# Later probabilities turned on TensorE, keys and values ahead of q, landings over both queues, a last product in two banks

## The chip, the cores and the metric

The kernel runs on one core of one Trainium2 chip. The metric is device time in microseconds of one execution; the median over runs counts. The engines have the profile's names: PE (TensorE, matrix products; PEld is its loading of weights), DVE (VectorE), ACT (ScalarE), POOL (GpSimd) and SP (SyncE, which here only issues transfers). Matrix products go into eight accumulation banks of 512 columns of 32-bit floats, from where DVE or ACT move them to on-chip memory; POOL cannot read the banks.

## The reference

All in 32-bit floats. First a linear attention, then a mixture of four experts in which every token goes through every expert.

```python
# attention: q, k, v are (8, 8, 576, 64)
kv  = np.einsum('bhsd,bhse->bhde', k, v)
out = np.einsum('bhsd,bhde->bhse', q, kv)
rms = np.sqrt(np.mean(out * out, axis=-1, keepdims=True) + 1e-06)
x   = out / rms * g_norm            # then (B, S, H*D) -> x: (4608, 512)

# experts: domain_probs (4608, 4), w1 (4, 512, 1024), w2 (4, 1024, 512)
p = domain_probs / (domain_probs.sum(-1, keepdims=True) + 1e-09)
for e in range(4):
    h = np.maximum(x @ w1[e], 0.0)
    out += p[:, e:e + 1] * (h @ w2[e])
```

## The kernel before

**Tiles and stages.** The 4608 tokens are nine chunks of 512: chunk `b` below 8 holds 512 tokens of batch `b`, the ninth the 64 left over from each of the eight batches. A step `s = 9 e + i` takes one chunk through one expert, so there are 36 steps. `opening` (L876) computes the attention of batch 0, `attention` (L1041) that of batches 1 to 7, one in each step of the first expert. The products of a step are `up` (x times w1) and `down` or `down_deep` (h times w2). They are written in Winograd's form of Strassen's scheme, seven products of half-size blocks instead of eight, in two levels where time allows; so DVE and POOL form sums and differences of weights and activations (`combine`, recorded at L579), ACT copies or negates, and half-products are merged from the banks. All matrix products of the steps are recorded at L556, in `halves_of`.

**Order of the work.** Nothing is ordered by the program text. Each piece of work is given to a planner (`Plan`, L44) by `plan.add`, with a key (about when), a cost for each engine that can do it, and its buffers. `layout` then simulates the core with these costs, once, when the kernel is built: it picks for every engine in turn the ready piece that is due first, and gives out buffers and banks as they become free. The order that results is the program, one queue for each engine, in which every instruction waits for all before it. In the simulation, `begin` (L352) reckons when a transfer lands: SP's transfers share one queue (`self.bus`), POOL's another (`self.bus_pool`), and neither knows of the other. `DEALS` is a table of draws for each step: each draw shifts the due times of some pieces at random, by a fixed generator, so another table is another order.

**The pieces that the change touches.** `norm_probs` (L592) loads the probabilities, four numbers (16 bytes) for each token, into `p_all`, with a token's block in the partition where the merge needs it. `load_first` takes those of chunk 0, `load_all` (L604 to L610) the rest, with seven transfers issued by POOL; `norm` (L613) divides by the sums. In `opening`, the four pairs of heads are loaded one after another by SP, q, then k, then v (L891). Four turns of q (L907), the product of keys and values (`key_values`, L918) and the turn of the ninth part of q (L926, in the same piece as the key and value product) lead to `attend` (L963). The weights of a later expert are loaded by SP; six of an expert's sums are started by ACT with a negated copy (`subtract_from`, L649, its ACT copy at L653), upon which POOL adds the other addend by a transfer that accumulates. `result` (L1588) gives `merge`, which scales half a product by a probability and adds it to the accumulator (on DVE at L1641, on ACT at L1633), and `send`, which writes a finished block to the output (L1657 by POOL, L1659 by SP). In the last step (`ends` in `down`, L1670) the last products go through a bank of kind `ab` with their merges behind them. At the start, while nothing is there to compute, PE runs products of the identity with itself (L1961).

## Time and profile before

| | |
|---|---|
| median of 3 runs | 1637.3 us (1635.74 to 1640.91) |
| the profiled execution | 1635.26 us, its span 1633.5 us |
| TensorE busy | 1622.3 us, 99% of the span |
| VectorE, ScalarE, GpSimd busy | 82%, 60%, 37% |
| transfers issued by SP (q1) | 199.96 MB, 40.3% of 16 engines' span |
| transfers issued by POOL (q0) | 36.78 MB, 15.0% |

The span runs from the first to the last instruction. A row of a group or of the order of time gives the engine, the line, the operation, tile written <- tiles read (buffer numbers left out), the shape and, after an x, how many instructions; in square brackets stands how long the engine was idle before, and whose work ended it. In the order of time the first two figures are start and duration in us; an instruction of PE counts until its result is out, so those that follow one another overlap in duration. `u`, `db`, `ab` are banks, `big`, `small`, `kv`, `xa`, `xb`, `w1y`, `w2y`, `w2e`, `snap` on-chip buffers.

### The profile page before, as it was taken

The numbers are of one execution on the slowest core, as the hardware profiler recorded it, in microseconds if no ns is written. First come the engines' busy times: TensorE is split into PE (matmuls) and PEld (weight loads), VectorE is DVE, ScalarE is ACT, GpSimd is POOL, SyncE is SP. The second block draws the span as 40 slices with busy tenths as digits, with TensorE's granted clock in tenths as the row PEclk, the third lists the DMA queues.
The fourth block names the chain that finished last, engine by engine and source line by source line (L and its number), as shares of the span: only waits on it lengthen the run. The fifth ranks groups of instructions, "written<-read, shape, count | busy, mean of one in ns | idle before, by whom it ended". The sixth has DMA issues, their size and how long they took to land.

```text
span 1633.5 us, 66413 instructions
## 1 busy us (share of the span) xinstructions
PE 1622.3 (99%) x28876; PEld 1555.9 (95%) x28876; DVE 1334.2 (82%) x2185; ACT 975.8 (60%) x2473; POOL 603.8 (37%) x581
## 2 busy tenths in 40 slices
PE   9999999999999999999999999999999999999999
PEld 5599888989999999999999999999999999999997
DVE  5877787888887987877988887878888887877876
ACT  4455655565566665665666666665566566666653
POOL 4111324232343545433454543332354533333333
PEclk9999999999999999999999999999999999999999
DMA  9977888653764435444676454344577544444442
GB/s 231 217 190 204 227 223 196 179 175 153 230 178 127 119 99 151 118 118 105 183 181 146 107 127 118 97 113 114 141 187 178 127 116 107 118 108 116 118 105 54
DMA packets 225598, 240.99 MB, mean 148 GB/s; under 512 B 100890, under 2 KB 165274, under 8 KB 225306
## 3 DMA queue, kind: packets, MB, share of 16 engines
q1 hardware_dynamic: 201690, 199.96, 40.3%
q0 software_dynamic: 23616, 36.78, 15.0%
q8 instruction: 227, 3.72, 0.9%
q14 instruction: 65, 0.53, 0.1%
HBM read 162.21 MB, written 74.47 MB: 145 GB/s over the span
## 4 chain that ended last, share of the span: by engine, by line
PE 97%; DMA 2%; SPq 0%; ACT 0%; issue 0%; DVE 0%; POOL 0%; DVEq 0%; ACTq 0%; POOLq 0%
PE u L556 47%; PE db L556 30%; PE ab L556 16%; PE ab L1113 1%; DMA big<-in_moe_w_dram 1%; PE ab L1138 1%; DMA big<-in_v_dram 1%; PE ab L1181 0%; DMA big<-roots 0%; SPq L585 0%; PE db L1138 0%; PE u L922 0%; PE ab L1961 0%; DMA kv<-in_v_dram 0%; PE db L963 0%
## 5 line engine op out<-in xcount | busy, mean ns | idle before, releaser
L579 DVE TENSOR_TENSOR big<-big,big 128x1024 f32<-128x1024 f32 (+1 forms) x572 | 537.8, 953 | 31.8 <-ACT big L1447 13.0
L556 PE MATMUL db<-big,big 128*64 128x128 f32 (+1 forms) x5344 | 400.4, 286 | 1.3 <-DVE big L579 0.7
L556 PEld LDWEIGHTS db<-big,big 128*64 128x64 f32 x5344 | 315.5, 137 | 22.1 <-ACT big L1633 2.1
L1491 DVE TENSOR_TENSOR big<-u,snap 128x256 f32<-128x256 f32 x460 | 193.6, 421 | 135.3 <-PE u L556 87.8
L1483 ACT ACTIVATE snap<-u 128x256 f32<-128x256 f32 x490 | 187.5, 383 | 165.1 <-PE u L556 134.2
L579 POOL TENSOR_TENSOR big<-big,big 128x256 f32<-128x256 f32 (+1 forms) x155 | 179.3, 1159 | 249.6 <-DVE big L579 150.5
L1483 ACT ACTIVATE big<-u 128x256 f32<-128x256 f32 x460 | 174.9, 383 | 74.2 <-PE u L556 54.6
L556 PE MATMUL u<-xa,big 128*64 128x128 f32 x2784 | 206.9, 273 | 0.0
L556 PE MATMUL u<-xb,big 128*64 128x128 f32 x2688 | 198.8, 273 | 0.0
L579 POOL TENSOR_TENSOR big<-big 128x512 f32<-128x512 f32 (+1 forms) x88 | 106.0, 1205 | 245.9 <-DVE big L579 136.7
L556 PE MATMUL u<-xa,w1y 128*64 128x128 f32 x2232 | 168.3, 273 | 1.8 <-ACT u L1483 1.8
L556 PEld LDWEIGHTS u<-xa,big 128*64 128x64 f32 x2784 | 163.4, 137 | 1.6 <-ACT big L1163 0.4
L556 PE MATMUL u<-xb,w1y 128*64 128x128 f32 x2208 | 164.7, 273 | 0.0
L1812 ACT ACTIVATE snap<-db 128x256 f32<-128x256 f32 (+1 forms) x256 | 91.6, 358 | 117.6 <-PE db L556 99.7
L556 PEld LDWEIGHTS u<-xb,big 128*64 128x64 f32 x2688 | 157.3, 137 | 0.1
L1447 ACT ACTIVATE big<-big 128x1024 f32<-128x1024 f32 x133 | 140.2, 1054 | 8.5 <-DVE big L579 7.5
L556 PEld LDWEIGHTS u<-xa,w1y 128*64 128x64 f32 x2232 | 131.1, 137 | 5.5 <-ACT u L1483 2.0
L556 PEld LDWEIGHTS u<-xb,w1y 128*64 128x64 f32 x2208 | 129.4, 137 | 0.5 <-DVE big L1641 0.4
L1820 DVE TENSOR_TENSOR big<-ab,snap 128x256 f32<-128x256 f32 x188 | 79.0, 420 | 61.9 <-ACT snap L1812 31.0
L1657 POOL DMA_DIRECT2D out_dram<-big x124 | 108.2, 1217 | 37.3 <-ACT big L1633 28.3
L579 DVE TENSOR_TENSOR big<-big 128x512 f32<-128x512 f32 (+1 forms) x155 | 116.6, 758 | 2.5 <-ACT big L1447 1.8
L1483 ACT ACTIVATE u<-u 128x256 f32<-128x256 f32 x245 | 90.9, 372 | 40.2 <-PE u L556 29.0
(244 smaller groups left out, 2849.6 us busy)
## 6 DMA issues: line engine op xcount, KB each, us to landing
xb<-x SPq DMA_DIRECT2D x44, 512.0 KB, 3.7
xa<-x SPq DMA_DIRECT2D x40, 512.0 KB, 3.5
out_dram<-big POOLq DMA_DIRECT2D x76, 256.0 KB, 6.1
big<-in_moe_w_dram SPq DMA_DIRECT2D x30, 512.0 KB, 5.8
w2e<-x SPq DMA_DIRECT2D x20, 512.0 KB, 3.9
xa<-x_h SPq DMA_DIRECT2D x37, 256.0 KB, 3.1
x_h<-big SPq DMA_DIRECT2D x18, 512.0 KB, 5.6
x<-xb SPq DMA_DIRECT2D x18, 512.0 KB, 4.5
```

The source lines that it names most:

```text
L556: nc.tensor.matmul(out_[cols], lhsT=lhsT[:, cols], rhs=rhs, **kw)
L579: lambda eng: adder(eng).tensor_tensor(out=out_(), in0=a(), in1=b(), op=op),
L1113: nc.tensor.matmul(bank.ap[o * D:(o + 1) * D, r * D:(r + 1) * D], lhsT=ks[r], rhs=vs[r], start=(j == r == 0), stop=(j == len(sets[0]) - 1) ...
L1138: nc.tensor.matmul(to[o].ap[cols, 0:width], lhsT=kv.ap[half, cols], rhs=qt.ap[half, r * S + at_:r * S + at_ + width],)
L1447: lambda eng: nc.scalar.activation(out=b.ap[:], in_=b.ap[:], func=ACT.Relu),
L1483: lambda eng: nc.scalar.activation(out=where(), in_=ps.ap[:, 0:HN], func=ACT.Copy),
L1491: lambda eng: nc.vector.tensor_tensor(out=block(whole, a, t), in0=src.ap[:, 0:HN], in1=add_.ap[:], op=ALU.add),
L1657: nc.gpsimd.dma_start(out=dst, in_=cell(i)[parts, :], accum_op=ALU.add)
L1812: lambda eng: nc.scalar.activation(out=where(), in_=group_of(ps.ap), func=ACT.Copy),
L1820: lambda eng: nc.vector.tensor_tensor(out=cell(tq, dq), in0=group_of(src.ap), in1=group_of(add_.ap), op=ALU.add,),
```

## The change

- **Probabilities.** Those of chunks 1 to 8 are loaded as 32 rows of 128 tokens (2 KB each) into a buffer of kind `big`: four transfers of seven rows (`load_rows`) and three for the four rows of left-over tokens (`load_ends`), all issued by POOL in two pieces. PE turns the rows, one transpose for each expert (`turn_all`), into a bank of kind `ab`, and DVE copies them to their places in `p_all` with five copies (`place_all`). `norm` follows as before.
- **Opening.** The loads of a pair of heads are issued as k, v, q. The planned sizes in the table beside them keep their places. The turn of the last part of q is a piece of its own, after the key and value product; the product no longer waits for q.
- **Landings.** In the simulation, a transfer on one queue is charged 1.2 times the time in which work of the other queue is under way beside it (`TOGETHER`), on both sides.
- **Last product.** In the last step, the second set of last products (t = 1) that use the first bank (m = 1, 6, 7) is cut into two of 128 columns, each in a bank of its own, with merges of 128 columns. The planned cost of a merge on DVE follows the width.
- **Draws.** The table `DEALS` is another one.

```diff
-    RATE, RATE_POOL, OPEN, MARGIN = 260.0, 130.0, 36.0, 1.0
+    RATE, RATE_POOL, OPEN, MARGIN, TOGETHER = 260.0, 130.0, 36.0, 1.0, 1.2
     DEALS = {
-        -3: (61,), -2: (115, 312), -1: (33, 472, 740, 903, 1097), 0: (62, 254, 593, 971, 1064), 1: (203,
...
+        -3: (139, 366), -2: (169, 421, 503, 934), -1: (223, 416, 853, 1011), 0: (151, 283, 537, 780, 1204),
...
         if eng == "SP":
-            self.bus = max(self.bus, t + 1.5) + op.kb / (215.0 if t < self.OPEN else self.RATE)
+            work = op.kb / (215.0 if t < self.OPEN else self.RATE)
+            self.bus = max(self.bus, t + 1.5) + work
+            if t >= self.OPEN:
+                self.bus += self.TOGETHER * min(max(0.0, self.bus_pool - self.bus + work), work)
...
             if op.kb:
-                self.bus_pool = max(self.bus_pool, op.end + 2.0) + op.kb / self.RATE_POOL
+                work = op.kb / self.RATE_POOL
+                other = min(max(0.0, self.bus - op.end - 2.0), work)
+                self.bus_pool = max(self.bus_pool, op.end + 2.0) + work + self.TOGETHER * other
...
-        def load_all(eng):
-            nc.gpsimd.dma_start(out=p_all[0:REM, B * NR, :], in_=first[:, S // D - 1, :])
-            nc.gpsimd.dma_start(
-                out=p_all[0:REM, B * NR + 1:NBLK, :], in_=by_batch[NT:S, 2::2, :])
-            nc.gpsimd.dma_start(out=p_all[REM:P, B * NR:NBLK, :], in_=by_batch[NT:S, 1::2, :])
-            for r in range(NR):
-                nc.gpsimd.dma_start(
-                    out=p_all[:, NR + r:B * NR:NR, :], in_=by_batch[r * P:(r + 1) * P, 1:, :])
+        def load_rows(eng):
+            t = rows_.ap[0:late, 0:P * E]
+            for r in range(NR):
+                nc.gpsimd.dma_start(
+                    out=t[r * (B - 1):(r + 1) * (B - 1), :],
+                    in_=whole[1:, r * P * E:(r + 1) * P * E])
+
+        def load_ends(eng):
+            ends, n = rows_.ap[NR * (B - 1):late, 0:P * E], REM * E
+            nc.gpsimd.dma_start(out=ends[:, n:], in_=whole[1::2, NT * E:])
+            nc.gpsimd.dma_start(out=ends[1:, 0:n], in_=whole[2::2, NT * E:])
+            nc.gpsimd.dma_start(
+                out=ends[0:1, 0:n].rearrange("p (x e) -> p x e", e=E),
+                in_=first[:, S // D - 1, :].unsqueeze(0))
+
+        def turn_all(eng):
+            t = rows_.ap[0:late, 0:P * E].rearrange("p (x e) -> p e x", e=E)
+            for e in range(E):
+                nc.tensor.transpose(
+                    bank.ap[:, e * late:(e + 1) * late], t[:, e, :], ident[0:late, 0:late])
+
+        def place_all(eng):
+            got = bank.ap[:, 0:late * E].rearrange("p (e n) -> p n e", e=E)
+            at = NR * (B - 1)
+            nc.vector.tensor_copy(out=p_all[:, B * NR:NBLK], in_=got[:, at:late])
+            for r in range(NR):
+                made = nc.vector.tensor_copy(
+                    out=p_all[:, NR + r:B * NR:NR], in_=got[:, r * (B - 1):(r + 1) * (B - 1)])
+            return made
...
-        plan.add(key + 0.8, {"POOL": 5.6}, load_all, writes=[probs_later], kb=72, after=opened, lands=5.5)
+        plan.add(key + 0.8, {"POOL": 3.5}, load_rows, parts=[rows_], kb=64, after=opened, lands=4.0)
+        plan.add(key + 0.9, {"POOL": 2.7}, load_ends, parts=[rows_], kb=16, after=opened, lands=4.0)
+        plan.add(key + 1.0, {"PE": 0.35}, turn_all, reads=[rows_], writes=[bank]).turns = True
+        plan.add(key + 1.1, {"DVE": 0.8}, place_all, reads=[bank], writes=[probs_later])
...
-            for t, src, kb in zip("qkv", (q, k, v), (
+            for t, src, kb in zip("kvq", (k, v, q), (
                     (172, 194, 290), (183, 150, 150), (237, 400, 150), (172, 150, 172))[hp]):
...
-                nc.tensor.transpose(bank[1].ap[0:D, P:2 * P], qt.ap[:, (J - 1) * D:J * D], ident[:])
-
-            turned = plan.add(
-                at(hp), {"PE": 1.28}, key_values, reads=[qt, kt, vt], writes=kbank)
+
+            turned = plan.add(at(hp), {"PE": 1.14}, key_values, reads=[kt, vt], writes=kbank)
             turned.turns = True
-            left_q = Buf(None, f"ql{n}")
+            left_q, turned_q = Buf(None, f"ql{n}"), Buf(None, f"qlt{n}")
+            plan.add(
+                at(hp), {"PE": 0.14},
+                lambda eng, bank=kbank, qt=qt: nc.tensor.transpose(
+                    bank[1].ap[0:D, P:2 * P], qt.ap[:, (J - 1) * D:J * D], ident[:]),
+                reads=[qt], writes=[turned_q], parts=kbank[1:], after=[turned]).turns = True
...
-                    key, {"DVE": 0.5},
+                    key, {"DVE": 0.14 + 0.0014 * (cols.stop - cols.start)},
...
+                cut = (P, P) if ends and t else (HN,)
                 if m == 1:
-                    banks[1] = Buf(kind, f"d1_{s}_{t}")
+                    banks[1] = [Buf(kind, f"d1_{s}_{t}_{w}") for w in range(len(cut))]
...
+                pieces = [
+                    (ps, slice(w * n, (w + 1) * n)) for w, (ps, n) in enumerate(zip(banks[1], cut))
+                ] if m in (1, 6, 7, 4) else [(banks[2], slice(0, HN))]
+
+                for ps, cols in pieces:
+                    wide = cols.stop - cols.start
...
```

More of the change, by code (lines that the diff above doesn't have):

```diff
@@ L1609, in rows, with cell @@
             ]
-        def cell(i, half=None):
+        def cell(i, half=None, cols=slice(0, HN)):
             at = (i % 2) * DM
@@ new lines, in down, with product @@
+                for ps, cols in pieces:
+                    wide = cols.stop - cols.start
+                    def product(eng, m=m, t=t, ps=ps, cols=cols, wide=wide):
+                        for kt in range(4):
+                            halves_of(
+                                ps.ap[:, 0:wide], four(h[m])[:, kt // 2, t, kt % 2, :],
+                                rhs=w2f[e][m].ap[:, kt * HN + cols.start:kt * HN + cols.stop],
+                                start=(m in (1, 2, 5) and kt == 0), stop=(kt == 3),
+                                skip_group_check=True,
+                            )
+                    op = plan.add(
+                        key, pe(4, wide), product, reads=[h[m], w2f[e][m], w2corner[e][m]],
+                        writes=[ps],
+                        after=(second[-1:] if m in (1, 5) and not ends else []) + firsts[t:t + 1],
+                    )
+                    op.marks, op.opens = (ps, wide), m == 1
+                    if m == 1 and cols.stop == HN:
+                        firsts.append(op)
+                    if m == order[-1]:
+                        second.append(op)
+                    to = [{
+                        1: (t, 0, True), 2: (t, 0, False), 6: (t, 1, True), 3: (t, 1, False),
+                        5: (2 + t, 1, True), 7: (2 + t, 1, 5 not in order), 4: (2 + t, 0, True),
+                    }[m]]
+                    if mixed and m == 5:
+                        to.append((t, 1, False))
+                    if mixed and m == 7:
+                        to.append((2 + t, 0, True))
+                    for i, half, fresh in to:
+                        merge(
+                            key - 0.4, [ps], lambda ps=ps, wide=wide: ps.ap[:, 0:wide], i, half,
+                            fresh, cols=cols)
```

42 lines of the change are left out of this document (9 added, 33 removed), and 10 rows, old and new, of the table DEALS.

## The prediction

> **What bounds the kernel now.** I read the page's busy times first, then the list of waits of TensorE, then busy time by stage, and last the order of time at the places where TensorE waits.
>
> ```profile
> PE 1622.3 (99%) x28876; PEld 1555.9 (95%) x28876; DVE 1334.2 (82%) x2185; ACT 975.8 (60%) x2473; POOL 603.8 (37%) x581
> ```
>
> TensorE is busy for 1622.3 of 1633.5 us. The arithmetic stays, so only the idle 11.2 us, and work of TensorE that is none, can be won. The waits (engine, line, what it waited for, total, times, longest):
>
> ```profile
> PE u L556 <- ACT u L1483: 1.8, 1, 1.8
> PE ab L1113 <- DMA big<-in_v_dram: 1.4, 1, 1.4
> PE ab L1961 <- POOL ident masks.py:199: 1.4, 1, 1.4
> PE u L556 <- DVE big L1491: 1.1, 1, 1.1
> PE db L556 <- DVE big L579: 0.7, 1, 0.7
> PE db L556 <- ACT big L1633: 0.6, 1, 0.6
> PE db L963 <- DVE kv L940: 0.3, 1, 0.3
> ```
>
> Seven waits, 7.3 us; nearly all the rest of the 11.2 lies behind the last matmul. By stage (after the stretch and its length stand the busy times of PE, PEld, DVE, ACT and POOL):
>
> ```profile
> 50.00:60.00 10.00, 10.00 (x132) 5.11 (x124) 9.81 (x19) 2.32 (x7) 0.00 (x0) 1.00 0.67 204
> 1200.00:1600.00 400.00, 399.98 (x7328) 399.70 (x7325) 323.95 (x519) 248.97 (x629) 154.77 (x145) 1.00 0.48 123
> ```
>
> In the late 400 us TensorE is never without work. In order of time the waits stand, as the rows below show, in the first 80 us and, one of them, at 857 us. So the answer is a sum over a few places.
>
> **1. Probabilities as rows.** Removed: seven POOL transfers, four of them (L610) in pieces of 16 bytes. Beside them stand loads of keys and values, before and during (KB each, median us from issue to landing):
>
> ```profile
> big<-in_k_dram SPq DMA_DIRECT2D x1, 240.0 KB, 4.2
> big<-in_v_dram SPq DMA_DIRECT2D x2, 240.0 KB, 8.4
> L610 POOL DMA_DIRECT2D p_all<-in_moe_domain_probs_dram x4: 943/952/995, 30.7 to 33.6; - x4
> 42.93 1.27 PE L1113 MATMUL ab<-big,big 120*64 120x64 f32 x36 [1.38 <-DMA big<-in_v_dram]
> ```
>
> The first row is from 24 to 29 us, the second from 29 to 43: the landing doubles while the four transfers of L610 are under way, and TensorE waits 1.38 us for just such a load of values. The price of the 16-byte pieces is thus up to 8.4 - 4.2 = 4.2 us of landing, more than the wait: with 2 KB rows I take the whole 1.4 us off (ends: 0, if the seven new transfers crowd as the old did; 1.4). What is late next is DVE. It waits for weights loaded behind the same crowd:
>
> ```profile
> 45.77 0.43 DVE L579 TENSOR_TENSOR w2y<-big 128x256 f32<-128x256 f32 x1 [2.42 <-DMA big<-in_moe_w_dram]
> 49.69 1.22 DVE L579 TENSOR_TENSOR big<-big,big 128x1024 f32<-128x1024 f32 x1 [1.18 <-DMA big<-in_moe_w_dram]
> 60.72 1.95 PE L556 MATMUL db<-big,big 128*64 128x256 f32 x16 [0.68 <-DVE big L579]
> ```
>
> DVE loses 2.42 + 1.18 us here, is then full from 50 to 60 us (9.81 of 10), and TensorE waits 0.7 us for a sum of its and 0.6 for a copy of ScalarE's. TensorE arrives 1.4 us earlier and DVE up to 3.6 us earlier, so the 1.3 us can go whole or stay; I take half, -0.6. The wait of 1.1 us on DVE L1491 at 77 us is left as it is.
>
> POOL still issues seven transfers (four of rows, three of ends) in place of seven (three and L610's four, 0.95 us each); I cost that at nothing either way, for POOL is the least busy engine (37%) and of the seven waits only the one for `ident`, at the very start, is for it. Added on TensorE: four transposes that turn 32 rows. The nearest row is the four transposes of 64 rows at L1019:
>
> ```profile
> 38.97 1.08 PE L556 MATMUL u<-big,big 128*64 128x512 f32 x4
> 39.98 0.46 PE L1019 MATMUL ab<-ident,big 64*128 64x64 f32 x4
> 40.37 1.08 PE L556 MATMUL u<-big,big 128*64 128x512 f32 x4
> 46.20 3.65 PE L556 MATMUL u<-big,big 128*64 128x512 f32 x16
> 39.95 0.18 DVE L617 RECIPROCAL inv<-inv 128x4 f32<-128x4 f32 x1
> ```
>
> From 38.97 to 40.37 is 1.40 us; the four 512-wide instructions in it take a quarter of the 16's 3.65, 0.9, so such a turn costs 0.5 with the change of form around it: I take +0.5 (ends +0.3 at half the rows, +0.8). The five small copies on DVE are 5 x 0.18 = 0.9 us of an engine that waits 3.6 us nearby: nothing, unless they fall between 50 and 60 us, where each tenth would be TensorE's. The one buffer of `big` and the bank of `ab` that are held meanwhile are costed at nothing, since the `ab` pair is used for attention only in this stage.
>
> **2. Keys and values ahead of q.** The first loads with their issue, their times to landing (the last figure), the first products, and the granted clock:
>
> ```profile
> 0.76 0.40 SPq L585 DMA_DIRECT2D big<-in_q_dram  x1
> 1.67 0.43 SPq L585 DMA_DIRECT2D big<-in_v_dram  x1
> big<-in_q_dram SPq DMA_DIRECT2D x1, 288.0 KB, 2.8
> big<-in_k_dram SPq DMA_DIRECT2D x1, 288.0 KB, 3.2
> big<-in_v_dram SPq DMA_DIRECT2D x1, 288.0 KB, 3.9
> 3.71 1.12 PE L907 MATMUL ab<-ident,big 128*128 128x128 f32 x4
> 6.09 1.95 PE L922 MATMUL u<-big,big 64*64 64x64 f32 x36
> 8.11 0.60 PE L907 MATMUL ab<-ident,big 128*128 128x128 f32 x4
> 9.36 1.23 PE L922 MATMUL u<-big,big 64*64 64x64 f32 x36
> PEclk9999999999999999999999999999999999999999
> ```
>
> Issued at 0.76, 1.67 and, k, halfway between, they land at 3.6 (q), 4.4 (k) and 5.6 (v). Now the four turns of q run while k and v are on their way (hidden), and the 36 products start at 6.09. After it the products can start at about 4.5 us, 1.6 earlier, but the turns then come behind them: 0.6 to 1.1 us by the two rows of L907. Gain 0.5 to 1.0. The left-over turn only changes place. From there to the wait on values TensorE has but the 0.3 us wait, so a start that is earlier stays earlier if the loads keep up; the loads in total are the same. I take -0.5 (ends -1.5 and +0.6, the turns in full with nothing gained because the weights still land when they did).
>
> The first 36 products take 1.95 us, the second 36 1.23: TensorE is slow at the start, while the granted clock stands at 9 tenths or more in the last row. The Trainium skill, "TensorE: Matmul & The Clock Gate", part 1, says that the array runs at half clock until a free-running window of about 3.4 us has been busy, and that the change of pace differs by half a microsecond between runs. By that rule the products moved ahead lie wholly in the slow time, so the opening would give about nothing, and the sum below would be half a microsecond smaller; the trace's two durations agree with half pace, and no row says where the window will fall.
>
> **3. Landings over both queues, and a new dealing.** The surcharge and the list of draws change no work, only the order on every engine. What it aims at shows at 855 us:
>
> ```profile
> 844.97 10.25 DMA big<-in_moe_w_dram
> 855.33 1.06 ACT L653 ACTIVATE big<-big 128x1024 f32<-128x1024 f32 x1 [3.06 <-DMA big<-in_moe_w_dram]
> 857.53 0.66 PE L556 MATMUL u<-xa,w1y 128*64 128x128 f32 x8 [1.76 <-ACT u L1483]
> ```
>
> A weight load took 10.25 us while POOL's transfers ran; ScalarE stood 3.06 us before its copy of it, the evacuations behind it waited, and TensorE 1.76. With landings reckoned later, that copy is ordered later: -1.8. But all positions are drawn anew, and the same kind of wait can turn up elsewhere: the old order has one in 1550 us, so I charge half a one, +0.9 (ends 0 and, for five more, below).
>
> **4. Last product in two banks.**
>
> ```profile
> 1627.60 1.90 PE L556 MATMUL ab<-big,big 128*64 128x256 f32 x16
> 1629.54 0.88 DVE L1641 SCALAR_TENSOR_TENSOR big<-ab,p_all,big 128x256 f32<-128x256 f32 x2 [0.85 <-PE ab L556]
> 1618.38 0.29 DVE L1820 TENSOR_TENSOR small<-u,snap 128x128 f32<-128x128 f32 x1
> 1616.34 0.61 PE L556 MATMUL u<-kv,big 128*64 128x128 f32 x8
> 1616.78 0.61 PE L556 MATMUL u<-w2y,big 128*64 128x128 f32 x8
> ```
>
> The two merges after the last matmul take 0.88 us. With the second half in a bank of its own, the first half's merges run beside the second half's products, and 2 x 0.29 = 0.6 us are left: -0.3 (ends 0 and -0.5). The products cost the same: eight 128-wide follow in 0.44 us, so 32 take 1.76, and 16 256-wide 1.73. A half's merge (0.3 us, beside 0.2 us of hand-over) fits into the other half's 0.87 us, so no wait is added between the products that share a bank.
>
> **The sum**, against the profiled execution's own 1635.26 us (span 1633.5 and 1.8 around it): -1.4 - 0.6 + 0.5 - 0.5 - 1.8 + 0.9 - 0.3 = -3.2, so 1632.1. That execution stands 2.0 us below the median of the runs shown, 1637.3; against the median the forecast is 1634.1, 0.2% less.
>
> **The rivals.**
> A. Every wait named goes, none comes: -1.4 - 1.3 - 1.1 - 1.8 - 1.0 - 0.4 + 0.5 = -6.5, 1630.8 (faster). For it: all but the 1.1 have one cause, late landings, that this change treats. Against it: DVE is full from 50 to 60 us.
> B. The change doesn't do what it says: new waits as large as the old take their places, as an order reckoned in advance cannot know each landing. Only turn, opening and tail are left, +0.5 - 0.5 - 0.3 = -0.3: 1637.0 (within).
> C. Slower: ScalarE's copies of weights (L653) stand in its queue ahead of the bank evacuations. There are six in each of three changes of expert, 18 in all, and one costs TensorE 1.76 us when its load is late. If the surcharge puts the loads later in SP's order, and the copies not, several meet it. From 3.2 + 4.9 = 8.1 us on, that is five of the 18, it decides: 5 x 1.76 = 8.8, 1642.9; seven give 1646.4. Against it: one of 18 does so now.
>
> **Chances.** Forecast 0.43, A 0.30, B 0.15, C 0.12. About 0.3% (4.9 us) is what a measurement of this kernel can tell from no change (the three runs lie 1635.74 to 1640.91). Faster is A, 0.30; slower is C, 0.12; within is the rest, 0.58. The range: down to A with the opening at its far end (0.5 more) and half of the 1.6 by which a run lies below the median, 1629.5; up to B with their scatter above it (3.6), 1640.6. C lies outside, and a little of A.
>
> **What would show it.** Right: loads of keys and values issued at about 33 us land in some 5 us instead of 8.4; no wait of L1113 on a load; the first L922 products before 5 us; no ScalarE wait near 3 us on weights; at the end two merges 128 wide after the last matmul. Busy time of TensorE stays within about 1 us of 1622 (the warm-up products at L1961 may change their number). Wrong: a new wait of TensorE above 2 us anywhere, which the list of waits shows, or a longer chain of DMA at a change of expert.

## The result and the profile after

The changed kernel takes 1633.14 us (median of 22 runs, 1631.04 to 1636.09), the kernel before 1636.12 us on the same chip (22 runs, 1633.76 to 1640.91). The ratio is 0.9981, 95% interval 0.9974 to 0.9987: 3.0 us less, a gain that is sure but smaller than the 0.3% that the prediction counted as a change. The forecast was 1634.1, reckoned from 1637.3, the median of the first three runs of the kernel before; the 22 runs have it 1.2 us lower.

The runs of one kernel lie 5 to 7 us apart, more than the change moves. So one profile of each kernel tells little about the sum, and here it misleads: the first profiled execution of the changed kernel took 1636.09 us, the slowest of its 22. It has these spans and busy times on its page:

```profile
span 1634.3 us, 66525 instructions
PE 1622.5 (99%) x28920; PEld 1559.9 (95%) x28920; DVE 1315.7 (81%) x2192; ACT 976.3 (60%) x2473; POOL 603.0 (37%) x583
```

TensorE's busy time is what it was (1622.3), so the difference is in its waits. From its list of waits in that execution, those of half a microsecond and more (engine, line, what it waited for, total, times, longest):

```profile
PE u L956 <- issue: 2.0, 1, 2.0
PE ab L2008 <- POOL ident masks.py:199: 1.4, 1, 1.4
PE u L561 <- ACT snap L1520: 1.2, 1, 1.2
PE u L956 <- DMA big<-in_v_dram: 0.9, 1, 0.9
PE db L561 <- ACT big L1670: 0.6, 1, 0.6
PE db L561 <- ACT snap L1859: 0.6, 1, 0.6
PE db L561 <- DVE big L584: 0.6, 1, 0.6
```

And the same list of a later execution of the very same kernel (the experiment `e11_after` below), which took 1631.87 us:

```profile
PE ab L2008 <- POOL ident masks.py:199: 1.4, 1, 1.4
PE db L561 <- DVE big L584: 1.1, 1, 1.1
PE u L956 <- DMA big<-in_v_dram: 0.7, 1, 0.7
PE db L561 <- ACT snap L1859: 0.6, 1, 0.6
PE db L561 <- ACT big L1670: 0.6, 1, 0.6
```

Two entries of the first list are not in the second: the 2.0 us before a product of keys and values (L956) for which the profile names no cause ("issue"), and the 1.2 us on a bank evacuation (L1520). All seven profiled executions of the two kernels together (three of before, four of after; waits of TensorE in us, from their lists of waits):

| | own time | first values | "issue" at 12 us | values at 42 us | DVE and ACT, 57 to 68 us | DVE at 77 us | evacuation at 858 us |
|---|---|---|---|---|---|---|---|
| before | 1635.26 | 0 | 0 | 1.4 | 0.7 + 0.6 | 1.1 | 1.8 |
| before (`e9_before`) | 1634.41 | 0 | 0 | 1.5 | 0.7 + 0.6 | 0.4 | 1.6 |
| before (`e12_before`) | 1639.37 | 0.7 | 0 | 2.6 | 0.7 + 0.6 | 0 | 1.4 |
| after | 1636.09 | 0.9 | 2.0 | 0 | 0.6 + 0.6 | 0 | 1.2 |
| after (`e1_again`) | 1634.19 | 1.0 | 1.2 | 0 | 1.2 + 0.6 | 0 | 1.1 |
| after (`e11_after`) | 1631.87 | 0.7 | 0 | 0 | 1.1 + 0.6 + 0.3 | 0 | 0 |
| after (`e13_after`) | 1633.51 | 0 | 0 | 0 | 1.5 + 0.6 + 0.7 | 0 | 0 |

Besides these, every profile of the changed kernel has one of 0.6 us near 90 us, two of the four have one of 0.4 or 0.9 us near 229 us, and the third one of before has one of 1.2 us near 121 us. All seven have 1.4 us at the very start and 0.2 or 0.3 us between 10 and 15 us.

To see where time was won and given back, I read at which time each execution had done the same work, counted in columns of TensorE's products from the start (the warm-up left out). Each figure is that time less the time in the second profile of before; a negative one is a lead:

| at (us, of before) | 10 | 18 | 35 | 45 | 75 | 100 | 840 | 870 | 1600 |
|---|---|---|---|---|---|---|---|---|---|
| before | 0.0 | 0.2 | 0.2 | 0.0 | 0.0 | 0.7 | 0.7 | 0.8 | 0.8 |
| `e12_before` | -0.1 | 0.4 | 0.4 | 2.9 | 4.4 | 3.8 | 5.2 | 5.0 | 5.0 |
| after | -1.1 | 2.8 | 2.9 | 1.0 | 1.7 | 1.2 | 2.6 | 2.4 | 2.2 |
| `e1_again` | -1.0 | 0.7 | 0.8 | -1.0 | 0.4 | 0.1 | 0.9 | 0.5 | 0.3 |
| `e11_after` | -0.8 | -0.4 | -0.4 | -2.2 | -0.5 | -1.0 | -0.1 | -1.8 | -2.0 |
| `e13_after` | -1.3 | -0.8 | -0.7 | -2.5 | -0.1 | -0.6 | 1.3 | -0.2 | -0.4 |

The orders differ, and a column of one kind of product costs more time than one of another, so single columns of this table are good to about 1 us: between 100 and 120 us, for one, all four executions of the changed kernel lose the same 1.06 us without a wait, which I put down to costlier products that stand later in its order, so that its leads up to 100 us look larger than they are. Four places differ by what happens there: 10 to 18 us (a lead is kept or lost), 35 to 45 us (1.8 us are won, in all four), 45 to 75 us (0.7 to 2.4 us are given back), and 840 to 870 us (0.2 to 1.7 us are won). After that nothing moves by more than 0.2 us.

### The profile page after: what moved, and what is told of

Its sections match the earlier page's. It is cut to its first block, busy times and chain, and to the rows that moved or that the text cites. A ratio compares the mean times of both kernels' runs of the same rounds, so it can differ in the third digit from the quotient of the medians.

```text
span 1634.3 us, 66525 instructions
## 1 busy us (share of the span) xinstructions
PE 1622.5 (99%) x28920; PEld 1559.9 (95%) x28920; DVE 1315.7 (81%) x2192; ACT 976.3 (60%) x2473; POOL 603.0 (37%) x583
## 4 chain that ended last, share of the span: by engine, by line
PE 97%; DMA 1%; DVE 1%; ACT 1%; SPq 0%; issue 0%; DVEq 0%; ACTq 0%
PE u L561 47%; PE db L561 31%; PE ab L561 16%; PE ab L1150 1%; PE ab L1175 1%; DMA big<-in_moe_w_dram 1%; PE ab L1218 0%; SPq L590 0%; DVE big L584 0%; PE db L1175 0%; DMA big<-in_v_dram 0%; PE u L956 0%; DMA kv<-in_k_dram 0%; PE db L1000 0%; ACT big L1670 0%
## 5 line engine op out<-in xcount | busy, mean ns | idle before, releaser
L584 DVE TENSOR_TENSOR big<-big,big 128x1024 f32<-128x1024 f32 (+1 forms) x546 | 484.5, 904 | 21.9 <-ACT big L1484 9.5
L561 PE MATMUL db<-big,big 128*64 128x128 f32 (+1 forms) x5576 | 418.6, 286 | 1.7 <-ACT big L1670 0.6
L561 PEld LDWEIGHTS db<-big,big 128*64 128x64 f32 x5576 | 333.7, 137 | 22.0 <-ACT big L1670 2.2
L1520 ACT ACTIVATE snap<-u 128x256 f32<-128x256 f32 x490 | 187.3, 382 | 157.1 <-PE u L561 125.1
L584 POOL TENSOR_TENSOR big<-big,big 128x256 f32<-128x256 f32 (+1 forms) x132 | 156.0, 1183 | 263.6 <-DVE big L584 131.8
L1520 ACT ACTIVATE big<-u 128x256 f32<-128x256 f32 x458 | 174.3, 382 | 80.3 <-PE u L561 61.6
L561 PE MATMUL u<-xa,big 128*64 128x128 f32 x2848 | 215.4, 273 | 1.2 <-ACT snap L1520 1.2
L561 PE MATMUL u<-xb,big 128*64 128x128 f32 x2816 | 214.6, 273 | 0.0
L561 PEld LDWEIGHTS u<-xa,big 128*64 128x64 f32 x2848 | 171.5, 137 | 3.8 <-issue 2.6
L561 PEld LDWEIGHTS u<-xb,big 128*64 128x64 f32 x2816 | 169.9, 137 | 0.1
L584 POOL TENSOR_TENSOR big<-big 128x512 f32<-128x512 f32 (+1 forms) x69 | 84.3, 1223 | 174.3 <-DVE big L584 104.1
L1484 ACT ACTIVATE big<-big 128x1024 f32<-128x1024 f32 x124 | 130.7, 1054 | 14.9 <-DVE big L584 11.8
L1520 ACT ACTIVATE u<-u 128x256 f32<-128x256 f32 x245 | 90.9, 371 | 39.5 <-PE u L561 26.7
```

The source lines that it names most:

```text
L561: nc.tensor.matmul(out_[cols], lhsT=lhsT[:, cols], rhs=rhs, **kw)
L584: lambda eng: adder(eng).tensor_tensor(out=out_(), in0=a(), in1=b(), op=op),
L1484: lambda eng: nc.scalar.activation(out=b.ap[:], in_=b.ap[:], func=ACT.Relu),
L1520: lambda eng: nc.scalar.activation(out=where(), in_=ps.ap[:, 0:HN], func=ACT.Copy),
```

## The experiments

My theory after the first profile: the wait on values and the tail came out as forecast; the opening's lead is lost in a stall that TensorE has at its 220th product; the wait at the change of expert is only made smaller. The rivals: the gain at 42 us comes from the new order and not from the 2 KB rows; the stall is chance; the landings' surcharge gives the whole gain.

### The changed kernel again

Unchanged.

> The changed kernel once more, unaltered, for a second profile. In the profile at hand, TensorE stood 2.0 us at 12 us with no wait shown and then ran 3.4 us at half clock; at equal work it was 1.2 us ahead of the kernel before at 10 us and 3.4 behind at 14 us. Theory 1: this is an accident of that execution (it is the slowest of 22, 3.0 us above their median); the second profile shows no such stall, its execution takes 1632 to 1634 us, and the opening keeps a lead of 1 to 1.5 us. Theory 2: the stall comes with the order of the changed kernel, as its first refill of instructions is asked for while the loads crowd the queue; the stall is there again within 0.5 us of the same place, and the median of 1633 already pays for it.

Measured: 1633.74 us, ratio 0.9976 (0.9967 to 0.9985, 12 runs). The stall at the 220th product was there, 1.2 us, and so were the waits at 60 and 858 us. The order of time of the first execution and of this one are alike at the stall; of the first:

```profile
4.49 1.26 PE L956 MATMUL u<-big,big 64*64 64x64 f32 x36
7.39 1.17 PE L956 MATMUL u<-big,big 64*64 64x64 f32 x33 [0.94 <-DMA big<-in_v_dram]
11.07 1.14 PE L956 MATMUL u<-big,big 64*64 64x64 f32 x29
14.25 0.53 PE L956 MATMUL u<-big,big 64*64 64x64 f32 x6 [2.04 <-issue]
```

The 36 products of keys and values start at 4.49 us (6.09 before), as planned. The next 36 wait 0.94 us for values. The third group breaks off within itself, where no product needs anything new.

### The old probabilities in the new order

```diff
         def load_rows(eng):
-            t = rows_.ap[0:late, 0:P * E]
             for r in range(NR):
                 nc.gpsimd.dma_start(
-                    out=t[r * (B - 1):(r + 1) * (B - 1), :],
-                    in_=whole[1:, r * P * E:(r + 1) * P * E])
+                    out=p_all[:, NR + r:B * NR:NR, :], in_=by_batch[r * P:(r + 1) * P, 1:, :])
...
         def turn_all(eng):
...
+            pass
...
         def place_all(eng):
...
+            pass
```

The three transfers of `load_ends` are again the three of before; every engine's order is that of the changed kernel.

> The changed kernel's own order on every engine, but the later probabilities come by the seven old transfers, four of them in pieces of 16 bytes, and nothing is turned or copied (TensorE's four transposes and five copies of VectorE fall away). Theory (forecast): loads of keys and values issued beside them land 3 to 4 us later, and TensorE waits 1 to 3 us for one of them or for VectorE's sums behind them before 65 us; less 0.5 us for the turn this is 0.5 to 2.5 us slower than the changed kernel. Rival: the order alone has moved the loads out of the way, and the wait of 1.4 us doesn't come back; then it is 0.3 to 0.5 us faster than the changed kernel, by the turn.

Measured: 1634.57 us, ratio 0.9987 (0.9979 to 0.9995, 12 runs), beside 1633.74 us and 0.9976 (0.9967 to 0.9985) of the changed kernel in the same comparison. By the medians the old form is 0.8 us slower, within the theory's range, though it is spared the turn; the two intervals overlap, and where the 0.8 us come from is not shown: it is not the theory's mechanism. What matters is that the wait on values at 42 us is gone here too. The four transfers with their times to landing, first in the old 16-byte pieces in this run, then as 2 KB rows in `e11_after`, then the landing of before:

```profile
L616 POOL DMA_DIRECT2D p_all<-in_moe_domain_probs_dram x4: 956/976/1164, 22.7 to 25.8; - x4
...
DMA to landing us min/median/max: 6.1/6.7/7.6
```

```profile
L617 POOL DMA_DIRECT2D big<-in_moe_domain_probs_dram x4: 518/538/704, 20.2 to 22.0; - x4
...
DMA to landing us min/median/max: 2.2/2.6/2.7
```

```profile
DMA to landing us min/median/max: 4.1/6.2/8.2
```

The rows do land sooner than the pieces, here by 4 us (their median is 2.3 to 4.5 us in the four executions of the changed kernel, for 6.7), and cost POOL half as much to issue (0.54 for 0.98 us). But in the new order POOL issues them at 20 to 26 us, while before it did so at 30.7 to 33.6, beside the loads of keys and values that TensorE needed at 42 us. Of the transfers issued from 29 to 43 us, those loads, in the run with the old pieces, in `e11_after` and in the first profile of the changed kernel (KB each, median us to landing):

```profile
big<-in_v_dram SPq DMA_DIRECT2D x2, 240.0 KB, 3.6
```

```profile
big<-in_v_dram SPq DMA_DIRECT2D x2, 240.0 KB, 4.5
```

```profile
big<-in_v_dram SPq DMA_DIRECT2D x2, 240.0 KB, 6.2
```

Instead of 8.4 us they take 3.6 with the pieces, and 3.6 to 6.2 with the rows in the four executions of the changed kernel. So the wait did not need the new form to go. Nor is the form enough, or the early issue by POOL: in `e5_qkv` below, another order with the rows issued at 19 to 21 us, the same load lands in 4.7 us and TensorE waits 1.45 us for it:

```profile
big<-in_v_dram SPq DMA_DIRECT2D x2, 240.0 KB, 4.7
```

```profile
41.89 1.29 PE L1150 MATMUL ab<-big,big 120*64 120x64 f32 x37 [1.45 <-DMA big<-in_v_dram]
```

There SP issues the load at 37.06 us, 2.6 us later than before (34.42). What is left is the order as a whole: when SP issues the load, what is under way beside it, and when TensorE comes to the product. In the changed kernel the product also stands later, 7.28 us behind the one of its kind before it, instead of 6.42 in the kernel before and in `e5_qkv`. How much each of these brings is not shown.

### The last product in one bank

```diff
-                cut = (P, P) if ends and t else (HN,)
+                cut = (HN,)
```

> The changed kernel with the last product in one bank; all else has the same order up to the last twenty us. Forecast: from the start of the last matmul group to the end of the span 0.3 us more (two merges 256 wide, 0.88 us, behind the last matmul instead of two of 128, 0.61), which the times cannot tell and the profile can. Rival: the end is set by the output's landing alone, and nothing changes.

Measured: 1633.72 us, ratio 0.9981 (0.9973 to 0.999, 10 runs), not to be told from the changed kernel. The traces tell it. The end of the changed kernel (first profile), then of this one:

```profile
1628.63 1.95 PE L561 MATMUL ab<-small,big 128*64 128x128 f32 x32
...
1630.61 0.61 DVE L1678 SCALAR_TENSOR_TENSOR big<-ab,p_all,big 128x128 f32<-128x128 f32 x2 [0.26 <-PE ab L561]
```

```profile
1627.04 1.90 PE L561 MATMUL ab<-small,big 128*64 128x256 f32 x16
1628.99 0.88 DVE L1678 SCALAR_TENSOR_TENSOR big<-ab,p_all,big 128x256 f32<-128x256 f32 x2 [0.85 <-PE ab L561]
```

From the first of these products to the end of the last merge it takes 2.59 us with two banks and 2.83 with one. Counted from the start of the last matmul to the end of the span it is 3.99 us (`e1_again`) and 4.35 (here): 0.2 to 0.4 us are won.

### The surcharge for the other queue left out

```diff
-    RATE, RATE_POOL, OPEN, MARGIN, TOGETHER = 260.0, 130.0, 36.0, 1.0, 1.2
+    RATE, RATE_POOL, OPEN, MARGIN, TOGETHER = 260.0, 130.0, 36.0, 1.0, 0.0
```

> The changed kernel with the surcharge for the other queue set to 0.0. The order is the same through the first expert and differs from the change to the second on, about 460 us. Theory (forecast): at one or more of the three changes of expert ScalarE waits 3 us or more on a weight load and TensorE 1.5 to 2 us, as before at 855 us; 1.5 to 4 us slower than the changed kernel. Rival: where TensorE waits is a matter of the draw, not of the surcharge; within 1 us of the changed kernel, with waits of TensorE behind 460 us of 0 to 2 us in total (now 1.2).

Measured: 1635.32 us, ratio 0.9992 (0.9981 to 1.0002, 12 runs), 1.6 us above the changed kernel in the same comparison (1633.74). The order stays the same up to about 460 us, so the gain at 42 us owes nothing to the surcharge. Later other waits take turns: none at 858 us, but 0.8 us near 487 us, where a copy of ScalarE waits 1.58 us for its weights (the theory had 3 us or more), and by the count of work 1.9 us are lost between 300 and 840 us and 1.8 won at 858. So the kernel is slower without the surcharge, at the near end of what the theory had; but since the draws were made with the surcharge, this does not measure its worth by itself, and that the wait at 858 us shrinks because of it is not shown, for it is gone without it too. What is telling in this profile is the clock. The stall and the window after it (stretch, its length, busy times of PE, PEld, DVE, ACT and POOL, then the granted clock):

```profile
13.54 0.39 PE L956 MATMUL u<-big,big 64*64 64x64 f32 x6 [1.18 <-issue]
```

```profile
15.00:17.00 2.00, 2.00 (x43) 1.62 (x45) 0.46 (x2) 1.55 (x3) 0.94 (x2) 0.50 1.06 385
```

The same 1.2 us stall as in `e1_again`, but here the granted clock of TensorE is at half afterwards, and there it stayed at 1.00.

### The opening and the draws taken back one at a time

The first with q, k, v, the second with the table `DEALS` of before, all else as changed:

```diff
-            for t, src, kb in zip("kvq", (k, v, q), (
+            for t, src, kb in zip("qkv", (q, k, v), (
```

> The changed kernel with q, k, v loaded in the old order; the planner makes a new order from it. Theory (forecast): the first products of keys and values start at 6 us instead of 4.4, and the kernel is 0.5 us slower than the changed one. Rival, from the second profile: the early start is lost by 14 us, because the instructions of TensorE run out at its 220th product (1.4 to 2.3 us in five of five profiles); with the products later, the refill comes in time, as in the kernel before, there is no such stall and no half clock behind it, and the kernel is 1 to 2 us faster than the changed one, if the rest of its order does no harm.

> The changed kernel with the table of draws of the kernel before; all four parts stay, the order is another from the opening on. Theory: the parts carry the gain; within 1.5 us of the changed kernel. Rival: the gain lies in the draws, chosen for this text; with others, waits of the size of those before come back (the stretch from 40 to 80 us and the change of expert at 855 us), 2 to 5 us slower than the changed kernel, at or above the kernel before.

Measured: 1649.85 us, ratio 1.0077 (1.0063 to 1.0091, 5 runs), and 1674.91 us, ratio 1.0231 (1.0217 to 1.0245, 4 runs). Both are far more than was expected. Both lose far from where they were edited, since the planner makes another order of everything from other loads or draws. The worst wait of each in the order of time:

```profile
381.56 0.66 PE L561 MATMUL u<-xa,w1y 128*64 128x128 f32 x8 [2.32 <-DVE xa L584]
```

```profile
171.09 1.98 PE L561 MATMUL db<-big,big 128*64 128x128 f32 x16 [16.37 <-ACT snap L1859]
```

In the second, a copy of ScalarE stands in the queue behind a load of q for 15.6 us, and TensorE behind it. So these two do not price the opening or the draws by themselves. In one point the rival of the first held: with q first the instructions come in time (its row in the table below), and TensorE does not stall near 12 us; the first products start at 5.33 us. The two show that the table of draws is worth tens of microseconds when it does not fit the rest, and that each part of such a kernel can only be tested with the order held, as in the old probabilities above.

### The stall near 12 us

Is it a place in TensorE's instruction stream (the sequencer waits for its next instructions), or a place in the work? Two kernels have the same opening behind a warm-up of fewer instructions, 84 less in each (the first, with 256 columns, also takes longer: 5.66 us, so that the first products start at 6.97 us instead of 4.49):

```diff
-        for r in range(4):
-            half = slice(r % 2 * D, (r % 2 + 1) * D)
-            nc.tensor.matmul(bank[half, 0:D], lhsT=ident[half, half], rhs=ident[half, half])
+        nc.tensor.matmul(
+            bank[:, 0:2 * P].rearrange("p (a t) -> p a t", a=2), lhsT=ident[:],
+            rhs=ident[:].unsqueeze(1).to_broadcast([P, 2, P]))
```

```diff
+        nc.tensor.matmul(bank[:, 0:P], lhsT=ident[:], rhs=ident[:])
```

> The changed kernel, but each of the seven warm-up groups is one product of 128 x 128 by 256 columns instead of four of 64 x 64 by 64: the same time of TensorE by its columns, 84 instructions fewer, and nothing else moves. Theory: TensorE's first store of instructions ends at about its 449th; with 84 fewer before, it ends some 40 products later, behind the landing of the refill at 13 us, so the stall at 12 us is gone or under 0.5 us, the half clock behind it too, and the kernel is 1 to 2 us faster than the changed one (1631.5 to 1632.5 against its 1633.7). Rival: the refill is asked for as much later as the store lasts longer; the stall stays at 1 us or more at the 449th instruction, and the time is the same.

> The kernel before once more, for a second profile. If the profile at hand is typical, its opening again reaches full pace by 8 us, has no stall at 12 us and the waits at 42, 60, 62, 76 and 855 us come back within 0.5 us each. If not, part of the gain is in waits that this profile did not show.

> The changed kernel with its fourteen warm-up groups as one 128x128 by 128-column product each, in place of four 64x64 ones: 84 TensorE instructions fewer ahead of the same opening, and each group about as long as before (the 256-column form took 0.40 us a group, four 64x64 ones 0.23). Theory 1 (the stall of 1.2 to 2.0 us at the 220th product is a refill of TensorE's instructions, tied to a place in the stream and done some 2.4 us after its 16-KB transfer starts): again the 220th product of the stream stalls, which is now 42 products later in the work. If that transfer is asked for by TensorE's progress (some 3 us after its 256th instruction, as with 256 columns), the stall stays at 0.5 to 1.5 us, near 14 us, and the time stays at that of the changed kernel, 1633 to 1635 us. Theory 2 (the transfer comes at 11 to 12 us whatever TensorE does): it has landed before it is needed, no stall is left, and the time falls by 1.2 to 1.7 us, to 1631.5 to 1632.5. Theory 3 (the stall has another cause, in the work itself): it stays at the same product of the keys, now the 178th of the stream, and as long.

> The changed kernel once more, beside the one with the short warm-up on the same chip: 1633 to 1635 us, 0.997 to 0.9985 of before, a stall of 1.2 to 2.0 us at the 220th product near 12 us. What differs between the two by less than 0.5 us cannot be told apart.

Measured: the 256-column warm-up 1633.77 us, 0.9982 (0.9973 to 0.9991, 10 runs); the 128-column one 1633.75 us, 0.9983 (0.9974 to 0.9992, 11 runs); the changed kernel beside it 1632.77 us, 0.9978 (0.9969 to 0.9987, 11 runs). No gain from either, though the first was expected to bring 1 to 2 us. The kernel before once more took 1634.41 us, without a stall; its waits came back within 0.2 us, but that at 77 us was 0.4 instead of 1.1. The changed kernel, run beside the second, had no stall this time, where 1.2 to 2.0 us were expected. But both kernels with the short warm-up stall, and again exactly after their 220th product, which is 42 products later in the work. In the 128-column one:

```profile
15.14 0.51 PE L1000 MATMUL db<-kv,big 64*64 64x64 f32 x19 [0.46 <-issue]
```

So the place is one in the instruction stream. The profile shows what belongs to it: transfers of 16 KB of kind "instruction" (queue q8). Over the whole span of the first profile they are

```profile
q8 instruction: 227, 3.72, 1.0%
```

and TensorE has 58184 records there, 227.3 for each 256; so I take this queue as TensorE's, 256 instructions in a transfer, which is an estimate. The first after the start is, in the first profile of the changed kernel from 11.8 to 13 us, and in `e11_after` from 8 to 10 us (packets, MB, share of the 16 engines):

```profile
q8 instruction: 1, 0.02, 5.0%
```

```profile
q8 instruction: 1, 0.02, 3.5%
```

| | instruction transfer starts | 220th product starts, the next starts | start of the next less that of the transfer | |
|---|---|---|---|---|
| after | 11.85 | 11.99, 14.25 | 2.40 | stall 2.0 |
| `e1_again` | 11.30 | 12.14, 13.53 | 2.23 | stall 1.2 |
| `e2_old_probs` | 11.30 | 11.77, 13.71 | 2.41 | stall 1.7 |
| `e3_tail_whole` | 12.14 | 12.90, 14.40 | 2.26 | stall 1.3 |
| `e4_no_together` | 11.19 | 12.14, 13.53 | 2.34 | stall 1.2 |
| `e5_qkv` | 9.07 | 11.78, at once | | none |
| `e6_old_draws` | 11.49 | 11.95, 13.83 | 2.34 | stall 1.7 |
| `e8_few_warm` | 13.65 | 15.47, 16.13 | 2.48 | stall 0.4 |
| `e10_short_warm` | 12.55 | 14.46, 15.14 | 2.59 | stall 0.5 |
| `e11_after` | 8.65 | 12.33, at once | | none |
| `e13_after` | 8.81 | 11.84, at once | | none |
| before, its three | 9.57, 9.67, 9.86 | 12.02, 11.94, 12.27, at once | | none |

(In us. Products, weight loads and the waits of its sequencer together, the 220th product is TensorE's 449th record in the trace; for those without a stall the middle column gives the start of that one. In `e6_old_draws` and in the kernel before it is the 221st product.) Whenever there is a stall, the next product comes 2.2 to 2.6 us after the transfer started; where the transfer started before 10 us, TensorE does not stall. In the three of before it was near: the 449th record starts 2.3 to 2.5 us after the transfer. Both theories of a refill were half right: the place is fixed in the stream, but the time of the transfer follows TensorE's progress only in part: it starts 2.8 to 3.7 us after the 256th instruction in the eight executions that stall and 0.1 to 1.5 us after it in the six that don't, among them `e11_after`, the same program as the first. The DMA engines are full at this time in all fourteen (share 1.01 to 1.09 in windows of 2 us from 10 to 16 us). What makes the transfer early or late, and whether the new order of loads makes it late more often, is not settled: it was late in six of eight executions with keys and values first and the old warm-up, and in none of four with q first (the three of before and `e5_qkv`). That speaks for the order of the loads; but two of the eight were early.

The Trainium skill, "Runtime: NRT & Kernel Launch", section "Instruction fetch mechanics", says that fetching the next block of instructions is mostly hidden; these traces show it hidden in six executions of the table and costing TensorE 0.4 to 2.0 us in eight.

### One more execution of each kernel

Both unchanged.

> One more look at the kernel before. If the transfer of TensorE's instructions comes early with q first (9.57 and 9.67 us in its two profiles) and late with keys and values first, it starts before 10 us again, and no stall of TensorE without a named cause is seen near 12 us; if it is early or late by chance, it can start after 11 us here too, with a stall of 1 us or more at the product that follows. The wait on a bank evacuation at 855 to 858 us (1.8 and 1.6 us in its two profiles) is there again if the order sets it, and can be gone if the landing of that execution does.

> One more look at the changed kernel. Its own time goes with the two places: with the instruction transfer before 9 us and no wait at 858 us, as in one profile so far, 1631.5 to 1632.5 us; with the transfer after 11 us and the wait there, as in the others, 1634 to 1636 us; with one of the two, in between.

Measured: 1639.37 us and 1633.51 us. In both the instruction transfer was early and nothing stalled. The kernel before was slow at another place, its wait on values:

```profile
44.44 2.26 PE L1113 MATMUL ab<-big,big 120*64 120x64 f32 x37 [2.62 <-DMA big<-in_v_dram]
```

```profile
44.00:46.00 2.00, 1.56 (x30) 1.59 (x32) 0.00 (x0) 0.00 (x0) 0.00 (x0) 0.50 1.10 346
46.00:48.00 2.00, 2.00 (x18) 0.83 (x15) 0.68 (x3) 0.28 (x1) 0.00 (x0) 0.50 1.08 341
48.00:50.00 2.00, 2.00 (x15) 0.80 (x16) 0.81 (x3) 0.00 (x0) 0.00 (x0) 0.50 1.11 217
```

The wait was 2.62 us instead of 1.4, and the granted clock then stood at half for more than 6 us. Together that put the execution from 0.45 us behind at 35 us to 4.4 behind at 60, by the count of work. The changed kernel has no wait there in its four profiles, its values landing 0.5 to 1.5 us before they are needed; a stall of the instructions, with the same fall of the clock behind it, is another way to a long execution, and one that it has. Its own time here missed the expectation: the transfer came before 9 us and nothing waited at 858 us, for which 1631.5 to 1632.5 us were expected; but it had waits of 0.9 us at 229 us and 2.8 us between 57 and 68 us.

## Why the prediction was right, and where not

The sum, -3.2 us, came out at -3.0 by the medians. Its terms did not all, so that it fits to 0.2 us is in part luck. What made up for the terms that failed is shown only in part: the kernel before has executions like `e12_before`, where the wait that is now gone cost more than the 1.4 us reckoned.

**The wait on values, -1.4: size right, reason wrong.** It is gone in every profile of the changed kernel; 1.8 us are won between 35 and 45 us. The step "with 2 KB rows I take the whole 1.4 us off" failed in its reason: the old 16-byte transfers in the new order take it off as well, and the rows in the order of `e5_qkv` leave 1.45 us of it. The first product that had to wait starts without a wait, here in the first profile of the changed kernel and in the run with the old pieces:

```profile
43.96 1.34 PE L1150 MATMUL ab<-big,big 120*64 120x64 f32 x40
```

```profile
43.42 1.34 PE L1137 MATMUL ab<-big,big 120*64 120x64 f32 x40
```

I had read the issue times of L610 (30.7 to 33.6) as a property of the pieces; they were a property of the order. That the size came out right is luck as far as the form goes.

**The waits on DVE and ScalarE near 60 us, -0.6: failed.** They stay, 1.2 to 2.8 us in place of 1.3. The step supposed that DVE would be earlier by as much as TensorE. It is not: weights still come late to it, and it is full before TensorE needs it (`e1_again`, first DVE by order of time, then the window with busy times of PE, PEld, DVE, ACT and POOL, then TensorE):

```profile
45.68 0.42 DVE L584 TENSOR_TENSOR w2y<-big 128x256 f32<-128x256 f32 x1 [2.36 <-DMA big<-in_moe_w_dram]
47.72 1.23 DVE L584 TENSOR_TENSOR big<-big,big 128x1024 f32<-128x1024 f32 x1 [0.94 <-DMA big<-in_moe_w_dram]
```

```profile
50.00:60.00 10.00, 9.74 (x88) 4.74 (x88) 9.93 (x23) 3.20 (x10) 0.74 (x1) 1.00 0.66 196
```

```profile
57.20 0.66 PE L632 MATMUL ab<-ident,big 32*128 32x32 f32 x4
60.90 1.95 PE L561 MATMUL db<-big,big 128*64 128x256 f32 x16 [1.16 <-DVE big L584]
```

DVE waits 2.36 us and 0.94 us for weights, where it waited 2.42 and 1.18, and is busy 9.93 of 10 us. So a TensorE that is early waits for it: the four executions lie between +1.0 and -2.5 us at 45 us, 3.5 apart, and between +1.7 and -0.5 at 75 us, 2.2 apart. Part of each gain ahead of 60 us is given back there.

**The turn, +0.5: right.** Four transposes of 32 rows take 0.59 us of TensorE (57.20 to the next at 57.79). The five copies fell where the prediction said they would cost something, at 58.8 to 59.3 us in `e1_again`, in the full stretch of DVE; but the run with the old pieces, which has no copies, waits there 1.0 us on DVE too, so their share is not shown.

**The opening, -0.5: right in two of four executions.** Where the instructions come early, the lead at 18 to 35 us is 0.4 to 0.8 us, as worked out. Where they come late, the lead of 1 us at 10 us turns into 0.7 to 2.9 us behind. (A wait of 0.7 to 1.0 us on the second pair's values, seen in three of the four, lies before 10 us and is taken off in that lead.) The step had "a start that is earlier stays earlier if the loads keep up" and looked at the loads of data alone; the wait that takes the lead away, 1.2 to 2.0 us, is for instructions (with 2.04 us in the first profile it is also the prediction's own sign of being wrong, a new wait above 2 us, which the other three do not have), and the half clock that can follow makes it dearer (first profile):

```profile
12.00:14.00 2.00, 0.21 (x8) 0.10 (x4) 0.56 (x2) 0.00 (x0) 1.54 (x3) 1.00 1.01 390
14.00:16.00 2.00, 1.75 (x12) 1.63 (x12) 0.00 (x0) 0.57 (x3) 0.64 (x1) 0.59 1.06 401
16.00:18.00 2.00, 2.00 (x55) 1.62 (x54) 0.45 (x2) 1.42 (x3) 0.73 (x1) 0.56 1.14 322
```

(0.41 + 0.44) x 2 / 0.5 = 3.4 us at half clock. That the products moved ahead would lie in the slow time, which the prediction had weighed, did not decide: the first 36 took 1.26 us in two executions and 1.73 and 2.09 in `e11_after` and `e13_after`, which gained all the same. In the kernel before they took 1.95, 1.87 and 1.27 us, so their pace is a matter of the execution. The row of the granted clock that the prediction set beside it has slices of 41 us and cannot show this.

**The change of expert, -1.8 + 0.9: right in sum.** The wait is 1.2, 1.1, 0 and 0 us in place of 1.8, 1.6 and 1.4, a gain of 1.0 on average, with a wait of 0.4 or 0.9 us elsewhere in two executions. The load and ScalarE's copy of it, in the first profile of the changed kernel and in `e11_after`:

```profile
848.59 8.88 DMA big<-in_moe_w_dram
```

```profile
857.56 1.06 ACT L687 ACTIVATE big<-big 128x1024 f32<-128x1024 f32 x1 [1.48 <-DMA big<-in_moe_w_dram]
```

```profile
853.23 1.05 ACT L687 ACTIVATE big<-big 128x1024 f32<-128x1024 f32 x1
```

The landing is shorter than the 10.25 us of before (10.1 and 9.9 in its other two profiles) and differs between executions of one order (8.9, 8.7, 6.9 and 7.7 us in the four). "No ScalarE wait near 3 us" on weights held: the longest is 1.5 in the four, after 3.1, 2.9 and 2.7 at this place before. The copy was not moved far enough behind the load to be safe in every execution, which the prediction had as all or nothing. That the surcharge brought this is not shown, as said above.

**The tail, -0.3: right**, 0.2 to 0.4.

**What the sum left at its old value:** the wait on DVE at 77 us (1.1 and 0.4 in two of three) is gone, one of 0.6 at 90 us is new: about even.

Rival A (all waits go, 1630.8) is near the shortest executions, 1631.0 to 1631.9, though by another sum: the waits near 60 us stayed in them too. Rival B was wrong as a whole, though a new wait did take the place of one removed, at the opening. Rival C did not come: no copy of ScalarE in the changed kernel waits for weights beyond 1.5 us.

## What to carry to other kernels

When a transfer is given a better form and is moved by the same change, test the form with the order held, for here the old form in the new order had no such wait either. A lead is worth what the next full engine lets through: look at whether that engine is early too before counting a second gain behind the first. And where a change moves less than the scatter between executions, take several profiles of each side and compare their waits place by place, since the first profile alone would here have given the change a loss of 0.8 us.

## What the runs showed of the hardware that I had not expected

TensorE can stall for its own instructions: 0.4 to 2.0 us at one place of the stream in eight of fourteen profiles, the next product 2.2 to 2.6 us after the start of a 16-KB instruction transfer, at a time when the DMA engines are full, and in some executions of a program and not in others.

A half clock can follow a stall that is not long. After 2.04 us of idle time the granted clock was at half for 3.4 us, after 1.72 us in `e2_old_probs` and 1.18 us in `e4_no_together` as well, and after 2.62 us for more than 6; after the same 1.18 us in `e1_again`, after 1.52 us in `e13_after` and after 1.76 us at 858 us in the kernel before it stayed at 1.00. So the length of the one wait does not decide. The Trainium skill, "TensorE: Matmul & The Clock Gate", part 1, describes a free-running window of about 3.4 us; the length of the times at half clock, 3.4 us and more than 6, agrees with one and two such windows. That it can follow an idle time of less than half of the window is from these runs.
